# Batch 0's last values ahead of gate 9, and two of their scalings on GpSimd

## Chip, core and metric

The kernel runs on one core of a Trainium2 chip. The metric is the device time of one execution in microseconds (us). Engines are named as in the profile: PE (matmul) with PEld (its weight loads), DVE (vector), ACT (scalar), POOL or GpSimd, SP (sync). ACT, SP and GpSimd also issue DMAs.

## What is computed

Attention in which a query sees 8 global keys and the 96 keys up to its own position, with a linear bias by distance, feeds a feed-forward block (SwiGLU). Cut to what matters:

```python
# q, k, v: (4 batches, 8 heads, 768 positions, 64), float32
scores = q @ k.T / sqrt(64) - slope[head] * dist      # outside the window: -1e9
a = exp(scores - max); a = a / sum(a)
x = (a @ v) -> (3072 tokens, 512)                     # heads side by side
g = x @ w_gate                                        # 512 x 1536
out = (g * sigmoid(g) * (x @ w_val)) @ w_out          # 1536 x 512
```

## The kernel before

**Tiles.** The 3072 tokens are eight tiles t of 384; batch b gives tiles 2b and 2b+1 (its two halves). Heads go in pairs (`hp` 0 to 3) and quads (`g` 0 and 1: pairs 0 and 1, pairs 2 and 3). Of a half, every quad needs its denominators (`den`: ones times the exponentials `at`), two numerators (`num`: values `vS` times `at`, one for each `side`), and then the scaling `xT = ns * rb`, where `ns` is ACT's copy of `num` and `rb` the spread reciprocal of `den`. The four slices of `xT` (index 2g + side) are the input of the feed-forward block of that tile.

**Feed-forward.** For each f of 12, *gate f* is four matmuls (`gps`, line 560 with `wg`, one for each slice of `xT`, in order); ACT makes `th`, DVE makes `sl` from `th` and `gps` (line 576). *Value f* is four matmuls (`vps`, line 560 with `wv`), and DVE makes `hT` from `vps` and `sl` (line 580). Output products (`ops`, line 592) come in four parts of three f each, and part p reads the p-th load of the third weights, `wo`.

**Order.** The order is written out by hand. Each engine carries out its instructions in the order of the program. For tile 0 it is the list `tile0`: a pair (f, 0) is gate f, (f, 1) value f, other entries are steps. DVE's work for later is kept in the list `later`; `run_later(n)` takes n pieces from it, mostly one ahead of each gate or value. `vas(0, 1)` calls `both_values(0, 1)`: denominators of both quads (each with DVE's transpose `dT`, line 462, and reciprocal), four numerators with ACT's copies (line 525), and four pieces for `later`: `spread_first` (quad 0's `rb`, line 468, and its two scalings, line 529), `spread` (quad 1's `rb`) and two `scale` (quad 1's scalings). For batch 0, all four scalings stand on DVE; for later batches, `spread_first` puts its two on GpSimd.

**PSUM banks.** Products of tile 0 rotate over three banks (`spare`: x0, x1, x2), attention over four (`bank`: a0 to a3). `widen` puts the four a-banks ahead of the three, and `narrow`, at tile 1, gate 2, takes them back. A bank is written again only when its reader, on DVE or ACT, is done.

**Queues.** All casting loads are issued by GpSimd, in program order, on one queue; each issue takes some 0.7 to 1 us of GpSimd and waits for the load issued eight before it. Ahead of tile 0's list, `late_loads` issues thirteen: the third part of `wo` (output weights 6 to 8), the global rows of k and v (`kG`, `vG`), the fourth part of `wo`, batch 1's second half of k and q (`kst`, `qst`), and batch 1's seven loads of v. Batch 2's loads follow from tile 1 on (`stage_rows`, `load_rows`). SP issues the copies from `vG` and `kG`, the transposes and the stores of the output.

Of the kernel before, what the change touches and what calls it, by code (L numbers as in the profile page):

```python
# [37 lines left out]
def kernel(  # L38
# [12 lines left out]
    nc = tc.nc  # L51
# [97 lines left out]
    def load_qk(b, h0, h1):  # L149
        for st, src in ((kst[b], k), (qst[b], q)):  # L150
            nc.gpsimd.dma_start(
                out=st[:, h0:h1, :],
                in_=src[b, h0:h1].rearrange("h (p j) d -> p h (j d)", p=128))
# [13 lines left out]
    def load_v_rest(b, c):  # L167
        n = min(KC, S - KC * c)
        nc.gpsimd.dma_start(  # L169
            out=vSs[b][NG:NG + n, c, :, :],  # L170
            in_=v[b, :, KC * c:KC * c + n, :].rearrange("h p d -> p h d"))
# [5 lines left out]
    def load_globals():  # L177
        for dst, src in ((kG, k), (vG[:, 1:], v)):
            nc.gpsimd.dma_start(
                out=dst.rearrange("p b h d -> p (b h) d"),  # L180
                in_=src[1:, :, 0:NG, :].rearrange("b h p d -> p (b h) d"))
# [33 lines left out]
    def load_wo(g):  # L215
        nc.gpsimd.dma_start(
            out=wo[:, 3 * g:3 * g + 3, :],
            in_=moe_w_out[384 * g:384 * g + 384].rearrange("(f p) d -> p f d", p=128))
# [11 lines left out]
    state = {"tags": ["a0", "a1", "a2", "a3"], "n": 0, "x": ["x0", "x1", "x2"]}  # L230

    def bank(name, dt=FP32):
        tag = state["tags"][state["n"] % len(state["tags"])]
        state["n"] += 1
        return single(name, tag, dt)

    def banks(name, dt=FP32):
        return [bank(name, dt) for _ in range(2)]

    def spare(name, dt=FP32):  # L240
        tag = state["x"][gv.get("n", 0) % len(state["x"])]
        gv["n"] = gv.get("n", 0) + 1
        return single(name, tag, dt)
# [11 lines left out]
    def run_later(n):  # L255
        for _ in range(n):
            if later:
                later.pop(0)()
# [254 lines left out]
    def both_values(b, half):  # L513
        two = [quads[b, g] for g in range(2)]
        for quad in two:
            den = spare("den") if b > 0 else bank("den")
            quad.weigh(half, den, None)
            quad.invert(den)
        srcs = {}
        for g, quad in enumerate(two):  # L520
            for side in range(2):
                num = spare("num") if b == 0 and g == 1 else bank("num")
                quad.weigh(half, num, side)
                src = sb2.tile([128, TB], FP32, name="ns", tag="ns", bufs=4)
                nc.scalar.copy(out=src, in_=num[:, 0:TB])  # L525
                srcs[g, side] = src

        def scale_num(eng, g, side):
            eng.tensor_mul(two[g].x_out(half, side), srcs[g, side], two[g].rb)  # L529

        def spread_first():
            two[0].spread()
            for side in range(2):
                scale_num(nc.gpsimd if b > 0 else nc.vector, 0, side)

        later.append(spread_first)
        def spread():
            two[1].spread()

        later.append(spread)  # L540
        for side in range(2):
            def scale(side=side):
                scale_num(nc.vector, 1, side)

            later.append(scale)
# [3 lines left out]
    gv = {}  # L549
# [157 lines left out]
    def late_loads():  # L707
        load_wo(2)
        load_globals()
        load_wo(3)  # L710
        load_qk(1, 4, 8)
        for c in range(NCH):
            load_v_rest(1, c)

    late_loads()

    gv["n"] = 1
    hb = [bank("gps") for _ in range(4)]

    def first_gates(*terms):  # L720
        for c, f in terms:
            products(0, f, 0, c, c + 1, hb[f])
# [20 lines left out]
    def vas(b, half):  # L743
        return lambda: both_values(b, half)
# [4 lines left out]
    def trh(h0, h1, by_pair):  # L749
        def step():  # L750
            b0, b1 = single("trs", "o0", FP16), spare("trs", FP16)
            (a, b), (c, d) = [(t[:, 0:TB], t[:, TB:2 * TB]) for t in (b0, b1)]
            if by_pair:
                jobs = [(h0, (b, a), A, A), (h1, (d, c), V, V)]
            else:
                jobs = [(h0, (c, a), V, A), (h1, (d, b), V, V)]
            for hp, tr, _, _ in jobs:
                pairs[0, hp].turn_half(1, tr)
            for hp, tr, k_eng, q_eng in jobs:
                pairs[0, hp].copy_half(1, tr, k_eng, q_eng)  # L760
        return step

    def sch(hp):
        def step():
            p = pairs[0, hp]
            for which in range(2):
                p.scores_half(1, which, banks("sc"), which == 1 and hp == 2, True)
            if hp == 2:
                later.insert(0, later.pop(1))
        return step  # L770
# [46 lines left out]
    first_gates(*[(c, f) for f in range(4) for c in range(2)])  # L817
    first_gates((2, 0), (2, 1), (2, 2), (3, 0), (3, 1), (2, 3), (3, 2), (3, 3))
    def late_widen():
        widen()  # L820

    def out_next():
# [2 lines left out]
    tile0 = [(0, 0), (1, 0), (2, 0), (3, 0), trh(0, 1, True), first_val(0), first_val(1),  # L825
             bias_of(0, 0), bias_of(0, 1), scores_of(0), (0, 1), (1, 1), (2, 1),
             trh(2, 3, False), sch(1), (3, 1), (4, 0), (5, 0), sch(2), (6, 0), (4, 1), (5, 1),
             (6, 1), sch(3), (7, 0), (7, 1), (8, 0), (9, 0), vas(0, 1), late_widen, (10, 0), (8, 1),
             (11, 0), (9, 1), (10, 1), out_next, (11, 1)]

    def ff(t, f0, f1, n_out=(0,)):
# [22 lines left out]
    for b, base, rate, v_at in ((2, 20, 2.0, (31, 32, 33, 34, 35, 36, 37)), (3, 38, 1.4, (56, 57, 58, 59, 60, 61, 62))):  # L854
        items = [(base, lambda b=b: stage_rows(b)), (base + 1, lambda b=b: load_ends(b))]
        n = 0
# [11 lines left out]
    def widen():  # L868
        x, n = state["x"], gv["n"]
        state["x"] = ([state["tags"][(state["n"] + i) % 4] for i in range(4)]  # L870
                      + [x[(n + i) % 3] for i in range(3)])
        gv["n"] = 0

    def narrow():
        assert gv["n"] % 7 == 3
        state["x"] = state["x"][4:]
        state["n"] += 3
        gv["n"] = 0

    at_step(1, 2, narrow)  # L880

    def take(step_list):
# [79 lines left out]
```

## Time and profile before

| | |
|---|---|
| median of 4 runs | 239.66 us (239.24 to 239.8) |
| profiled execution, its own time | 239.80 us |
| its span in the profile | 238.0 us |
| PE busy | 231.9 us, 97% |
| DVE, ACT, POOL busy | 169.7, 127.4, 94.0 us |
| granted PE clock | full throughout |
| one scaling (line 529) on DVE, on GpSimd | 556 ns, 994 ns |

How to read it: times in the profile are in us from the start of the span. In a timeline line, the first number is the start, the second the duration of the merged group, then engine, line of the code, operation, output <- inputs, shapes, and the count (x4). In brackets stands how long the engine was idle ahead of it, and what ended that. The rows of page part 2 are forty slices of the span, each digit tenths of busy time.

### The profile page before, as it was taken

The page shows a single profiled execution, that of the slowest core. Times are in us where ns is not written, and L with a number is a line of the kernel's source. Part 1 is how long each engine was busy: PE and PEld are TensorE (multiplying, and loading weights), DVE is VectorE, ACT ScalarE, POOL GpSimd, SP SyncE. Part 2 cuts the span into 40 slices and gives each one's busy share as a digit, 9 for nine tenths or more (in the row PEclk, how much of TensorE's full clock was granted, in tenths as well). Part 3 has the DMA queues.
Part 4 walks back from the last instruction along what each step waited for, and adds up shares of the span by engine and source line. Part 5 has one row for each costly group of instructions (what it writes and reads, how often), then busy time and mean ns, then how long its engine had stood idle before and what let it go on. Part 6 is the DMA issues. An engine that isn't in the chain of part 4 may idle for free.

```text
span 238.0 us, 6012 instructions
## 1 busy us (share of the span) xinstructions
PE 231.9 (97%) x2406; PEld 134.1 (56%) x2406; DVE 169.7 (71%) x372; ACT 127.4 (54%) x290; POOL 94.0 (39%) x113
## 2 busy tenths in 40 slices
PE   7999999999999999999999999999999999999994
PEld 4665465655555556555655556555655566555543
DVE  6878889968896778676884768685885568555530
ACT  4886775687837275367347275367346526233311
POOL 8976574665990004993082063600032213000000
PEclk9999999999999999999999999999999999999999
DMA  7999999999999346999049459910010110111022
GB/s 138 171 195 200 186 200 204 196 165 160 156 152 142 97 113 93 132 134 147 4 66 114 108 113 131 134 50 21 27 44 5 42 44 3 45 47 44 8 81 90
DMA packets 83332, 25.00 MB, mean 105 GB/s; under 512 B 72600, under 2 KB 80360, under 8 KB 83304
## 3 DMA queue, kind: packets, MB, share of 16 engines
q0 software_dynamic: 64208, 14.05, 68.5%
q1 hardware_dynamic: 18664, 10.36, 17.5%
q8 instruction: 19, 0.31, 0.5%
q10 hardware_dynamic: 432, 0.21, 0.4%
q14 instruction: 9, 0.07, 0.1%
HBM read 28.62 MB, written 6.29 MB: 147 GB/s over the span
## 4 chain that ended last, share of the span: by engine, by line
PE 87%; DMA 7%; POOL 3%; ACT 1%; issue 0%; DVE 0%; POOLq 0%
PE gps L560 26%; PE vps L560 25%; PE ops L592 25%; DMA wg<-in_moe_w_gate_dram 7%; PE num L452 3%; PE sc L392 3%; PE den L452 2%; PE trs L272 1%; POOL vS L169 1%; PE ops L608 1%; POOL k L118 1%; ACT at L367 1%; POOL q L118 1%; POOL wg L211 0%; PE sc L356 0%
## 5 line engine op out<-in xcount | busy, mean ns | idle before, releaser
L571 ACT ACTIVATE th<-gps 128x384 f32<-128x384 f32 x96 | 47.3, 494 | 61.8 <-PE gps L560 57.2
L560 PE MATMUL gps<-xT,wg 128*128 128x384 f16 x384 | 78.0, 327 | 1.0 <-DMA wg<-in_moe_w_gate_dram 0.3
L576 DVE SCALAR_TENSOR_TENSOR sl<-th,gps 128x384 f32<-128x384 f32 x96 | 52.7, 551 | 36.7 <-ACT th L571 36.1
L560 PE MATMUL vps<-xT,wv 128*128 128x384 f16 x384 | 77.6, 326 | 0.3 <-DMA wv<-in_moe_w_val_dram 0.3
L592 PE MATMUL ops<-wo,hT 128*128 128x512 f16 x276 | 73.1, 379 | 0.0
L580 DVE TENSOR_TENSOR hT<-vps,sl 128x384 f16<-128x384 f32 x96 | 52.8, 554 | 7.8 <-PE vps L560 0.6
L560 PEld LDWEIGHTS <-wg 128*128 128x128 f16 x384 | 35.4, 98 | 32.6 <-issue 2.7
L560 PEld LDWEIGHTS <-wv 128*128 128x128 f16 x384 | 37.2, 98 | 26.0 <-DMA wv<-in_moe_w_val_dram 0.9
L592 PEld LDWEIGHTS <-hT 128*128 128x128 f16 x276 | 26.9, 98 | 23.7
L400 ACT ACTIVATE at<-sc 128x432 f16<-128x432 f32 x72 | 33.9, 533 | 10.3 <-PE sc L392 10.3
L529 POOL TENSOR_TENSOR xT<-ns,rb 128x384 f16<-128x384 f32 x10 | 9.8, 996 | 63.4 <-ACT ns L525 32.1
L169 POOL DMA_DIRECT2D vS<-in_v_dram x28 | 24.8, 899 | 4.7 <-DMA kst<-in_k_dram 2.0
L598 ACT ACTIVATE osb<-ops 128x512 f32<-128x512 f32 x23 | 13.7, 597 | 14.3 <-PE ops L592 14.1
L411 POOL TENSOR_TENSOR at<-at,masks 128x864 f16<-128x864 f16 x4 | 7.3, 1821 | 23.9 <-ACT at L400 19.3
L411 DVE TENSOR_TENSOR at<-at,masks 128x864 f16<-128x864 f16 x20 | 12.2, 609 | 5.4 <-ACT at L400 5.4
L192 POOL DMA_DIRECT2D kst<-in_k_dram x16 | 14.1, 901 | 3.5 <-DMA vS<-in_v_dram 2.4
L525 ACT COPY ns<-num 128x384 f32<-128x384 f32 x24 | 9.8, 494 | 9.9 <-PE num L452 9.9
L192 POOL DMA_DIRECT2D qst<-in_q_dram x16 | 13.8, 889 | 0.3 <-PE trs L272 0.3
L367 ACT ACTIVATE at<-sc 128x432 f16<-128x432 f32 (+2 forms) x32 | 11.4, 462 | 1.5 <-PE sc L356 1.5
L408 DVE TENSOR_TENSOR at<-at,masks 128x432 f16<-128x432 f16 x24 | 8.1, 377 | 4.1 <-ACT at L400 4.1
L452 PE MATMUL num<-at,vS 128*32 128x216 f16 (+6 forms) x576 | 10.9, 224 | 0.0
L462 DVE STREAM_TRANSPOSE dT<-den 128x384 f32<-128x384 f32 x16 | 9.3, 581 | 1.2 <-PE den L452 0.5
(72 smaller groups left out, 164.9 us busy)
## 6 DMA issues: line engine op xcount, KB each, us to landing
out_dram<-osb SPq DMA_DIRECT2D x23, 256.0 KB
vS<-in_v_dram POOLq DMA_DIRECT2D x24, 120.0 KB, 5.4
wg<-in_moe_w_gate_dram POOLq DMA_DIRECT2D x6, 256.0 KB, 9.5
wv<-in_moe_w_val_dram POOLq DMA_DIRECT2D x6, 256.0 KB, 8.2
wo<-in_moe_w_out_dram POOLq DMA_DIRECT2D x4, 384.0 KB, 10.2
qst<-in_q_dram POOLq DMA_DIRECT2D x16, 96.0 KB, 4.3
kst<-in_k_dram POOLq DMA_DIRECT2D x16, 90.0 KB, 4.4
kst<-in_k_dram POOLq DMA_DIRECT2D x2, 384.0 KB, 10.8
```

The costliest lines, as they stand in the source:

```text
L169: nc.gpsimd.dma_start(out=vSs[b][NG:NG + n, c, :, :], in_=v[b, :, KC * c:KC * c + n, :].rearrange("h p d -> p h d"))
L192: nc.gpsimd.dma_start(out=st[b][p0:p0 + n, h // 2, :, h % 2, :], in_=src[b, h, 0:n * J].rearrange("(t p) d -> p t d", p=n))
L367: nc.scalar.activation(out=at[:, hi, 0:col + n], in_=sc[hi][:, 0:col + n], func=AF.Exp, scale=scale)
L400: nc.scalar.activation(out=at[:, hi, :], in_=sc[hi][:, 0:BANK], func=AF.Exp, scale=scale)
L411: mul_eng.tensor_mul(at, at, m[:, :, o:o + BANK])
L452: nc.tensor.matmul(dst[r, o:o + n], lhsT=ones[:, 0:32] if side is None else vals[:, 4 * g + j, side::2], rhs=pairs[b, 2 * g + j // 2].at[c ...
L560: nc.tensor.matmul(gv[f, which][:, 0:TB], lhsT=w[:, c, 128 * f:128 * f + 128], rhs=x_of(t)[:, c, :], start=(c == 0), stop=(c == NC - 1))
L571: nc.scalar.activation(out=th, in_=dst[:, 0:TB], func=AF.Tanh, scale=0.5)
L576: nc.vector.scalar_tensor_tensor(out=sl, in0=th, scalar=1.0, in1=dst[:, 0:TB], op0=AluOp.add, op1=AluOp.mult)
L580: nc.vector.tensor_mul(hTs[t][:, f, :], dst[:, 0:TB], gv.pop(("sl", f)))
L592: nc.tensor.matmul(ops, lhsT=hTs[t][:, f, 128 * i:128 * i + 128], rhs=wo[:, f, :], start=(f == 0), stop=(f == NFF - 1))
L598: nc.scalar.mul(out=osb, in_=ops, mul=0.5)
```

## The change

Three things move. In `spread_first`, the two scalings of quad 0 are given to GpSimd for batch 0 as well. `late_loads()` is no longer called ahead of tile 0's list, but in `late_widen`, after `run_later(1)` has issued `spread_first`; on GpSimd the thirteen loads therefore stand behind the two scalings. In `tile0`, gate 9 moves from ahead of `vas(0, 1)` to behind `late_widen`, so that PE carries out denominators and numerators right after gate 8. As one product less is on the three banks by then, and one more on the seven, `narrow` counts four used banks instead of three.

```diff
         def spread_first():
             two[0].spread()
             for side in range(2):
-                scale_num(nc.gpsimd if b > 0 else nc.vector, 0, side)
+                scale_num(nc.gpsimd, 0, side)
...
-    late_loads()
-
...
     def late_widen():
+        run_later(1)
+        late_loads()
         widen()
...
-             (6, 1), sch(3), (7, 0), (7, 1), (8, 0), (9, 0), vas(0, 1), late_widen, (10, 0), (8, 1),
+             (6, 1), sch(3), (7, 0), (7, 1), (8, 0), vas(0, 1), late_widen, (9, 0), (10, 0), (8, 1),
...
     def narrow():
-        assert gv["n"] % 7 == 3
+        used = gv["n"] % 7
+        assert used <= 4
         state["x"] = state["x"][4:]
-        state["n"] += 3
+        state["n"] += used
         gv["n"] = 0
```

In the built program, DVE's order after gate 8's `sl` becomes: `dT` and reciprocal of both quads, both spreads, gate 9's `sl`, a scaling of quad 1, gate 10's `sl`, the other scaling, value 8's `hT`. On GpSimd an instruction of the library (profiled as MODIFY_POOL_CONFIG), which the build places ahead of the first multiply on that engine, moves with it: before, it stands ahead of batch 1's scalings, behind the third load of batch 2's v; after, ahead of batch 0's scalings, behind the first half of batch 1's q.

## The prediction

> **What bounds the kernel now.** I read the page first (busy time, slices), then the timeline around the edit, then GpSimd's own timeline and the rows of line 529.
>
> ```profile
> PE 231.9 (97%) x2406; PEld 134.1 (56%) x2406; DVE 169.7 (71%) x372; ACT 127.4 (54%) x290; POOL 94.0 (39%) x113
> ...
> PEclk9999999999999999999999999999999999999999
> DMA  7999999999999346999049459910010110111022
> ```
>
> PE is the bound, at full clock; the other engines matter only where PE waits for them. The DMA engines are full until about 77 us. The timeline from 30 to 40 us:
>
> ```profile
> 30.62 0.81 PE L560 MATMUL gps<-xT,wg 128*128 128x384 f16 x4
> ...
> 31.16 0.55 DVE L576 SCALAR_TENSOR_TENSOR sl<-th,gps 128x384 f32<-128x384 f32 x1 [0.43 <-ACT th L571]
> ...
> 31.63 0.60 DVE L373 TENSOR_TENSOR at<-at,masks 128x864 f16<-128x864 f16 x1
> 31.77 0.81 PE L560 MATMUL gps<-xT,wg 128*128 128x384 f16 x4 [0.33 <-DVE sl L576]
> ...
> 32.51 0.79 PE L452 MATMUL den<-at,ones 128*32 128x72 f16 x40
> ...
> 32.62 1.07 DVE L576 SCALAR_TENSOR_TENSOR sl<-th,gps 128x384 f32<-128x384 f32 x2
> ...
> 33.13 1.39 PE L452 MATMUL num<-at,vS 128*32 128x72 f16 x80
> ...
> 34.45 0.82 PE L560 MATMUL gps<-xT,wg 128*128 128x384 f16 x4
> ...
> 34.55 0.58 DVE L462 STREAM_TRANSPOSE dT<-den 128x384 f32<-128x384 f32 x1
> ...
> 35.19 0.81 PE L560 MATMUL vps<-xT,wv 128*128 128x384 f16 x4
> ...
> 37.95 1.03 DVE L529 TENSOR_TENSOR xT<-ns,rb 128x384 f16<-128x384 f32 x2
> ...
> 39.08 0.81 PE L560 MATMUL gps<-xT,wg 128*128 128x384 f16 x4
> ```
>
> Gate 8 is at 30.62, gate 9 at 31.77, gate 10 at 34.45, value 8 at 35.19, tile 1's first gate at 39.08. Four matmuls take 0.65, so PE was ready for gate 9 at 31.27 and stood 0.50 us: its bank was gate 7's, which DVE's sl frees at 31.71. That is all the idle time to be won here. From 34.45 on PE has next to no gap.
>
> GpSimd's timeline, then the rows of line 529 on GpSimd:
>
> ```profile
> 32.02 0.74 POOL L151 DMA_DIRECT2D qst<-in_q_dram  x1
> 32.75 0.74 POOL L216 DMA_DIRECT2D wo<-in_moe_w_out_dram  x1
> ...
> 41.20 0.95 POOL L169 DMA_DIRECT2D vS<-in_v_dram  x1 [1.25 <-DMA kst<-in_k_dram]
> 43.12 0.94 POOL L169 DMA_DIRECT2D vS<-in_v_dram  x1 [0.98 <-DMA qst<-in_q_dram]
> 44.98 3.58 POOL L169 DMA_DIRECT2D vS<-in_v_dram  x4 [0.92 <-DMA wo<-in_moe_w_out_dram]
> ```
>
> ```profile
> L529 POOL TENSOR_TENSOR xT<-ns,rb x10: 992/994/1002, 92.6 to 199.0; 128x384 f16<-128x384 f32 x10
> ...
> L529 POOLq MODIFY_POOL_CONFIG  x2: 112/112/113, 71.3 to 71.3; - x2
> ```
>
> Two things to see. Each load waits for the one issued eight before it, so the right-hand notes date landings: kst of 31.11 by 41.20, qst of 32.02 by 43.12, wo of 32.75 by 44.98. At 32.75 some 10 us of transfers stand in line. And ahead of GpSimd's first multiply of the whole program stands a library load, two MODIFY_POOL_CONFIG at 71.3, as soon as the issues before it are out (71.4). The first multiply comes at 92.58, so 21 us cover it.
>
> [...]
>
> **The change part by part.**
>
> *Gate 9 behind the values.* The stall of 0.50 goes, and two others take its place. After gate 8 PE goes straight to the denominators: 31.27 plus the change-over (0.09: 32.51 against 31.77 + 0.65), 31.36. Quad 0's twenty take 0.31, the first ten of quad 1's 0.12: 31.80. The eleventh reads pair 3's second half, whose mask (31.63 + 0.60) is ready at 32.23. Before, PE came there at 32.95, too late to notice; now it stands until 32.28, with all 80 numerators and gate 9 queued behind. The last ten end at 32.47, the 80 numerators take 1.32: gate 9 starts at 33.79 in the bank of quad 0's denominator. DVE frees that in time: one sl instead of two (0.52 less) lies ahead of its transposes, so they run at 33.09 and 34.03 instead of 33.61 and 34.55. Gate 10 takes quad 1's bank, free at 34.61: PE, ready at 34.45, starts at 34.67, and value 8 at 35.33, against 35.19. **Sum: 0.14 us late**, give or take 0.1. Nor could more be won: value 8's second half of weights lands only at 35.1 to 35.4 (GpSimd's wait for it ended ahead of 35.41), and its third matmul starts at 35.51 now, so at most 0.35 of gain.
>
> *Bank bookkeeping.* Seven banks in another rotation, four used instead of three: no instruction, and each bank's last reader is over by then. 0.
>
> *Two scalings from DVE to GpSimd.* DVE is spared 2 x 0.55, from 35.9. No PE wait lies there (its ones are in time even now: 37.95 + 1.03 against 39.08), so 0. On GpSimd they need quad 0's spread, ready at 35.31 (0.52 earlier than 35.83), and ACT's copies, earlier too: 35.4 to 37.35 if nothing else holds them. PE needs the first at 39.22, the second with the next matmul at 39.38: 2 us of room.
>
> *The library load.* In the built order of the changed kernel it stands ahead of these scalings, behind the qst issue of 32.02. So it starts at 32.76, and the 21 us of cover become 2.6. With a length L the scalings end at 32.76 + L + 1.95, and PE, 0.05 later, loses 32.76 + L + 2.00 - 39.38 = **L - 4.62**. From both sides: nothing up to 4.6[...]. I take 8.5[...]: **3.9 us**.[...] PE is 97% busy and back to back afterwards, so nothing gives this back.
>
> *The loads issued behind.* wo's third part, kG, vG, wo's fourth, the second kst and qst, seven vS, with batch 2's rows behind them, go from 32.75 to behind the scalings: 37.35 without the load, 43.2 at L = 8.5. The line of transfers lasts to about 43, so in the first case nothing lands later: the wait for eight before holds vS at 41.20 anyway. In the second the line runs dry and landings move by some 2.5 us; readers move by 4. wo's third part is read at 46.5 now, 1.8 after landing (44.7 to 45). 0, as long as PE is later than the transfers. SP's copies from vG wait until 50.35 anyway.
>
> *Sum.* 0.14 + 3.9 = 4.0 on the profiled execution's 239.80, 243.84. That execution stands 0.14 above the median of 239.66, so I forecast **243.7**.
>
> **Rivals.**
>
> 1. *Not slower: the library load is short, or done ahead.* For it: nothing in the records shows its length, and the first multiply at 92.58 starts in the moment its inputs are there. Against: that was 21 us later, which says nothing below 21. It decides at L = 4.6 us. Then only gate 9's move is left, between 0.35 won and 0.25 lost: 239.3 to 239.9, likeliest 239.8.
>
> 2. *No library cost, but late weights hold PE.* If a transfer takes its 12 us from issue (32.75 to 44.98) instead of its place in line, wo's third part, issued at 37.35, lands at 49.6 and PE, which reads it at 46.5, loses 3.1: 242.9. Against: the landings are 1.9 us apart, as in a line.
>
> 3. *DVE is the hidden bound and the 1.1 us come back.* Against: from 34.45 PE runs without gaps, so there is nothing to take; at most rival 1's lower end.
>
> **How the numbers follow.** A measurement here tells about 0.2%, 0.5 us, from no change. The library load in the open[...]: 0.78, times of 241.1 to 248.8. Rival 1: 0.14, nearly all within 0.2%. Rival 2: 0.05. Rival 3 or faster for a reason not seen: 0.03. So slower 0.83, same 0.13, faster 0.04.[...]
>
> **What would show it.** Right: MODIFY_POOL_CONFIG near 32.8, the first line 529 on GpSimd at about 41 and not 35.4; PE's gate of tile 1 waiting for POOL xT L529 by some 4 us; denominators stopped by the mask of line 373 near 32.3; value 8 near 35.3. Wrong: scalings at 35.4 (no library cost), or a PE wait for DMA wo at 46 to 50 (rival 2), or PE idle elsewhere.

## The result and the profile after

The changed kernel takes 240.01 us (median of 43 runs, 239.37 to 240.54) against 239.61 for the kernel before (64 runs): a ratio of **1.0014, interval 1.0008 to 1.002**. It is slower, but by about 0.34 us by that ratio (the two medians are 0.40 apart), and not by the 4 us of the forecast. The profiled execution took 239.95 us with a span of 238.2.

The page of the changed kernel, busy time and the DMA slices:

```profile
PE 231.7 (97%) x2406; PEld 134.2 (56%) x2406; DVE 169.4 (71%) x370; ACT 127.7 (54%) x290; POOL 96.3 (40%) x115
...
DMA  8999999999999474999049459910010110111022
```

PE does the same 2406 matmuls and its share is unchanged. The DMA slices differ from those of before in the first one and from 77 to 95 us (4, 7, 4 tenths instead of 3, 4, 6), where PE's digits stay at 9. The loss is too small for the page. It is seen in the timeline of the changed kernel around the edit (start, duration, engine, line, operation, count, idle time ahead and its releaser):

```profile
30.46 0.81 PE L560 MATMUL gps<-xT,wg 128*128 128x384 f16 x4
...
31.20 0.69 PE L452 MATMUL den<-at,ones 128*32 128x72 f16 x30
...
32.12 0.34 PE L452 MATMUL den<-at,ones 128*32 128x216 f16 x8 [0.23 <-DVE at L373]
...
32.33 1.11 PE L452 MATMUL num<-at,vS 128*32 128x72 f16 x61
...
33.65 0.45 PE L452 MATMUL num<-at,vS 128*32 128x192 f16 x15 [0.20 <-issue]
...
34.03 1.47 PE L560 MATMUL gps<-xT,wg 128*128 128x384 f16 x8
...
35.29 2.27 POOL L529 TENSOR_TENSOR xT<-ns,rb 128x384 f16<-128x384 f32 x2 [2.19 <-DVE rb L468]
35.34 0.81 PE L560 MATMUL vps<-xT,wv 128*128 128x384 f16 x4
...
37.51 0.79 POOL L216 DMA_DIRECT2D wo<-in_moe_w_out_dram  x1
...
39.24 0.81 PE L560 MATMUL gps<-xT,wg 128*128 128x384 f16 x4
```

Gate 8 itself starts at 30.46 here and at 30.62 before: its time differs by some tenths from profile to profile (29.93 to 30.62 in all of them). So I read everything as time after gate 8, written with a plus sign. Gate 9 starts at +3.57, value 8 at +4.88 (before +4.57), tile 1's first gate at +8.78 (before +8.46). **The loss of 0.31 us is complete at value 8 and only carried from there.** The lines show two stops on the way: the denominators wait for the mask of line 373 until 32.12, and the last 15 numerators start at 33.65, after a stop that no engine and no transfer ends ("issue").

The rows of line 529 on GpSimd, changed kernel (duration min/median/max in ns, first and last start):

```profile
L529 POOL TENSOR_TENSOR xT<-ns,rb x12: 991/996/1307, 35.3 to 199.1; 128x384 f16<-128x384 f32 x12
...
L529 POOLq MODIFY_POOL_CONFIG  x2: 37/37/37, 33.1 to 33.1; - x2
```

The scalings run at 35.29, with MODIFY_POOL_CONFIG, the library load of the forecast, at 33.1 ahead of them. There is no load in the open, which was the main term of the forecast: the wait of 2.19 ahead of the scalings ends with `rb`.

### The profile page after: what moved, and what is told of

It reads as the page before. It is cut to its first block, busy times and chain, and to the rows that moved or that the text cites. A ratio compares the mean times of both kernels' runs of the same rounds, so it can differ in the third digit from the quotient of the medians.

```text
span 238.2 us, 6015 instructions
## 1 busy us (share of the span) xinstructions
PE 231.7 (97%) x2406; PEld 134.2 (56%) x2406; DVE 169.4 (71%) x370; ACT 127.7 (54%) x290; POOL 96.3 (40%) x115
## 4 chain that ended last, share of the span: by engine, by line
PE 87%; DMA 7%; POOL 3%; ACT 1%; issue 1%; DVE 0%; POOLq 0%
PE gps L560 26%; PE vps L560 25%; PE ops L592 25%; DMA wg<-in_moe_w_gate_dram 7%; PE num L452 4%; PE sc L392 3%; PE den L452 2%; PE trs L272 1%; POOL vS L169 1%; PE ops L608 1%; POOL k L118 1%; ACT at L367 1%; POOL q L118 1%; POOL wg L211 0%; PE sc L356 0%
## 5 line engine op out<-in xcount | busy, mean ns | idle before, releaser
L560 PEld LDWEIGHTS <-wg 128*128 128x128 f16 x384 | 35.4, 98 | 32.0 <-issue 2.1
L529 POOL TENSOR_TENSOR xT<-ns,rb 128x384 f16<-128x384 f32 x12 | 12.1, 1022 | 65.6 <-DVE rb L468 54.7
```

Of the source, the lines that this page charges most:

```text
L560: nc.tensor.matmul(gv[f, which][:, 0:TB], lhsT=w[:, c, 128 * f:128 * f + 128], rhs=x_of(t)[:, c, :], start=(c == 0), stop=(c == NC - 1))
```

## The experiments

The theories after this result: **T1**, the loss is gate 9's move alone, through the two stops; **T2**, the scalings or the loads issued behind them cost something; **T3**, MODIFY_POOL_CONFIG does start a load that takes its time, but it hides between 33.1 and 35.29.

### Each half alone

e1_gate_only undoes what was done to GpSimd, e2_gpsimd_only what was done to gate 9.

```diff
 # e1_gate_only, against the changed kernel
-                scale_num(nc.gpsimd, 0, side)
+                scale_num(nc.gpsimd if b > 0 else nc.vector, 0, side)
...
+    late_loads()
...
         run_later(1)
-        late_loads()
         widen()
```

> Only gate 9 moves behind batch 0's last values; the two scalings stay on DVE and the thirteen loads keep their old place. Theory (the order on PE is the whole loss): as slow as the full change, 1.0014 of before (0.2 to 0.5 us), with gate 9 starting about 3.6 us after gate 8 and value 8 about 4.9 us after it (4.57 before), a hold in the denominators at the mask of line 373, and a stop of about 0.3 us inside the last numerator. Rival (GpSimd's scalings, its library instruction or the later loads are the loss): no slower than before, within 0.1 us.

```diff
 # e2_gpsimd_only, against the changed kernel
-             (6, 1), sch(3), (7, 0), (7, 1), (8, 0), vas(0, 1), late_widen, (9, 0), (10, 0), (8, 1),
+             (6, 1), sch(3), (7, 0), (7, 1), (8, 0), (9, 0), vas(0, 1), late_widen, (10, 0), (8, 1),
```

> Only the scalings go to GpSimd and the loads behind them; gate 9 stays ahead of the values. Theory (order on PE is the loss, GpSimd and loads are hidden): within 0.1 us of before, scalings start as soon as quad 0's rb is ready, PE has the stall of 0.5 us ahead of gate 9 and no stop in the numerators. Rival (late loads or GpSimd cost something): 0.2 to 0.4 us slower than before, with a PE wait for POOL xT or for DMA wo.

Measured: e1 1.0013 [1.0003, 1.0024], e2 0.9993 [0.9984, 1.0003]. PE's timeline in e1:

```profile
30.22 0.81 PE L560 MATMUL gps<-xT,wg 128*128 128x384 f16 x4
...
33.38 0.45 PE L452 MATMUL num<-at,vS 128*32 128x192 f16 x15 [0.17 <-issue]
33.77 1.47 PE L560 MATMUL gps<-xT,wg 128*128 128x384 f16 x8
```

Gate 9 at +3.55 and value 8 at 35.08, +4.86: e1 repeats the changed kernel's numbers with both stops in it, the one in the last 15 numerators too. In e2 value 8 is at +4.57 and tile 1's gate at +8.46, as before. So the whole loss is gate 9's move; scalings and loads on GpSimd cost nothing that can be measured (at the upper end of e2's interval, 0.07 us). T2 falls.

### The library load

Two multiplies of ones are put on GpSimd directly behind batch 1's first half of q, ahead of the scalings, so that they need nothing that could hide a load.

```diff
 # e3_lib_probe, against the changed kernel
     load_qk(1, 0, 4)
+    probe = sb.tile([128, 2, 64], FP16, name="probe")
+    for i in range(2):
+        nc.gpsimd.tensor_mul(probe[:, i], ones[:, 0:64], ones[:, 64:128])
```

> The full change with two more small multiplies (128x64, of a constant tile, result unused) on GpSimd, right behind the library instruction and ahead of the scalings; their input is ready since the start, so the time from MODIFY_POOL_CONFIG to the first of them is the library load itself, with the DMA engines full. If the load is long but hidden in the change by the wait for rb: the first multiply starts 1 to 2.2 us after MODIFY_POOL_CONFIG. If nothing is loaded: within 0.3 us. If the first call is what costs: it is much longer than the second.[...]

One run, 239.95 us. The rows of the added line on GpSimd in e3:

```profile
L708 POOLq MODIFY_POOL_CONFIG  x2: 37/37/37, 33.4 to 33.4; - x2
L708 POOL TENSOR_TENSOR probe<-ones x2: 309/312/316, 33.5 to 33.7; 128x64 f16<-128x64 f16 x2
```

The first multiply follows the two MODIFY_POOL_CONFIG within 0.1 us, and the two take the same time (309 to 316 ns). T3 falls: in this program nothing of that length stands behind the instruction.

### The stop in the numerators

The stop has no releaser, and it stands at the same place, 15 numerators ahead of gate 9, in the changed kernel, in e1, in e3 and below in e5. That points at the instructions themselves. Page part 3 has 19 packets of 16 KB in a DMA queue of kind "instruction" (q8): here instructions arrive in blocks. I took this queue to be PE's, whose 2 x 2406 records would then be some 253 to a packet, an estimate from the page; e4 tests it. If PE ran out of instructions, moving the block's border by other instructions should remove the stop, or move it. e4 makes 44 short warm-up products of 12 long ones: 64 more PE instructions (a weight load and a matmul for each of 32 more products), at the start of the program.

```diff
 # e4_shift, against the changed kernel
-            nc.tensor.matmul(warm[:, 0:256], lhsT=ones[:, 0:128], rhs=ones[:, 0:256],
+            nc.tensor.matmul(warm[:, 0:64], lhsT=ones[:, 0:128], rhs=ones[:, 0:64],
...
-    fill(12)
+    fill(44)
```

> The full change with the 12 warm-up matmuls of 256 columns at the start cut into 44 of 64 columns: same array time, but 64 more instructions ahead on PE, so every later 16 KB packet of PE's instruction stream[...] starts 64 instructions earlier in the work. Theory (the stop inside the last numerator is PE waiting for its next packet of instructions): the stop of 0.3 us goes, or moves to another place; gate 9 comes about 0.3 us earlier after gate 8 (3.3 us), gate 10 then waits some 0.2 us for DVE's dT of quad 1, and the whole is 0.1 to 0.2 us faster than the full change. Rival (the stop belongs to the numerators themselves, a bank or a value load): it stays where it was, gate 9 at 3.6 us after gate 8.

Measured: 239.67 us, ratio 1.0003 [0.9988, 1.0018]. The interval holds both the time of before and that of the changed kernel, so the reading rests on the trace. The timeline of e4:

```profile
30.23 0.81 PE L560 MATMUL gps<-xT,wg 128*128 128x384 f16 x4
...
32.10 1.38 PE L452 MATMUL num<-at,vS 128*32 128x72 f16 x76
...
33.42 1.66 PE L560 MATMUL gps<-xT,wg 128*128 128x384 f16 x8
...
34.92 0.81 PE L560 MATMUL vps<-xT,wv 128*128 128x384 f16 x4
```

The last 76 numerators go through in 1.38, without a stop. Gate 9 starts at +3.19, gates 9 and 10 take 1.66 instead of 1.47 because gate 10 now waits for quad 1's `dT`, and value 8 is at +4.69. The DMA view of the stretch from 29 to 34 us in the changed kernel, and then of 24 to 29 us in e4 (packets, MB, share):

```profile
q8 instruction: 1, 0.02, 1.2%
```

```profile
q8 instruction: 1, 0.02, 1.1%
```

In the changed kernel the block's packet is on its way from 31.36 to 32.29 and the instructions taken to be its own run at 33.65; in e4 the packet is there by 26.4, and none comes from 29 to 34. This also tells whose packet it is: e4 adds instructions to PE alone, and q8's packet comes 5.9 us earlier, while the 8 KB packets of the other instruction queue (q14) keep their places near 24.5 and 30.2. It fits a block that is asked for at a fixed earlier instruction: 64 instructions of gates and values are some 5 us of PE's time (eight of them take 0.65), those of denominators and numerators less than one. The kernel before has the late packet as well (to 32.36), but PE comes to that place only at about 34.0, 1.7 after the packet's end, and does not notice. Why the instructions run only 1.4 us or more after their packet's end, the runs don't show.

To know what the same edit does to the kernel before, it was run there too.

> The kernel before with the warm-up in 44 pieces alone: control. There PE reaches row 962 of its instructions later than their packet, so nothing is to be won: ratio 1.000 within 0.001, value 8 at 4.57 us after gate 8. If cutting the warm-up gains by itself (an earlier start), it shows here and has to be taken off the two kernels above.

e8_before_shift: 239.52 us, 1.0003 [0.999, 1.0016], value 8 at +4.56 and tile 1's gate at +8.46. So what e4 has over the changed kernel at value 8 (+4.69 against +4.88) comes with the stop and not from the warm-up as such. These are single profiles: e3, the changed kernel with a shorter stop, has value 8 at +4.77.

### Taking the stops away one by one

e5 gives DVE pair 3's second mask one item earlier, ahead of gate 7's `sl`; e6 adds e4's edit; e7 also gives gate 9 the bank of gate 8, so that gate 10 no longer waits for quad 1's `dT`.

```diff
 # e5_mask_first, against the changed kernel
             run_later(3)
+        elif item == (7, 0):
+            run_later(2)
 # e7_mask_shift_rot: also e4's edit, and in widen and narrow
-        state["x"] = ([state["tags"][(state["n"] + i) % 4] for i in range(4)]
-                      + [x[(n + i) % 3] for i in range(3)])
+        xs = [x[(n + i) % 3] for i in range(3)]
+        state["xs"] = xs[1:] + xs[:1]
+        state["x"] = (xs[:1] + [state["tags"][(state["n"] + i) % 4] for i in range(4)]
+                      + xs[1:])
...
-        state["x"] = state["x"][4:]
-        state["n"] += used
+        state["x"] = state["xs"]
+        state["n"] += used - 1
```

> The full change with pair 3's second mask (line 373) one piece earlier in DVE's order, ahead of gate 7's sl, so that it is ready before PE's denominators reach it. If the hold at the mask were a loss by itself, gate 9 would come 0.4 us sooner after gate 8 (3.57 us in the full change). Expected instead: the hold goes and nothing is gained, gate 9 again at 3.4 to 3.6 us after gate 8, since the last loads of batch 0's values (vS, landing near 32.2 and 32.4) stop the first numerator and PE's instructions from row 962 on stop the last one, as before.

PE's timeline in e5 (one run, 239.79 us), with two lines of its weight loads (PEld) in between:

```profile
31.02 0.79 PE L452 MATMUL den<-at,ones 128*32 128x72 f16 x40
...
32.00 0.10 PEld L452 LDWEIGHTS <-vS 128*32 128x32 f16 x4 [0.21 <-DMA vS<-in_v_dram]
...
32.26 0.75 PEld L452 LDWEIGHTS <-vS 128*32 128x32 f16 x49 [0.15 <-DMA vS<-in_v_dram]
...
33.40 0.45 PE L452 MATMUL num<-at,vS 128*32 128x192 f16 x15 [0.22 <-issue]
33.78 1.47 PE L560 MATMUL gps<-xT,wg 128*128 128x384 f16 x8
```

The wait for the mask is gone: 40 denominators in 0.79. Gate 8 was at 30.28, and gate 9 is still at +3.50, as expected. PE comes to the numerators about 0.4 earlier and loses it again in two places: the loads of `vS`, the values of batch 0, end two short waits (0.21 and 0.15), and PE then stands before the same instruction as in the changed kernel, 0.46 from one numerator's start to the next instead of 0.40. The three lie one behind the other, and taking the first away brings out the next.

> The same with the warm-up in 44 pieces, so that no packet of instructions is missing in the numerators. Expected: no stop in the last numerator, a short wait of the first numerator for vS, gate 9 about 3.05 us after gate 8; gate 10 then waits for DVE's dT of quad 1 and value 8 stays at about 4.6 to 4.7 us. If the packets were not the cause of the stop in the last numerator, gate 9 stays at 3.4 or later.

PE's timeline in e6 (one run, 239.35 us):

```profile
32.21 1.29 PE L452 MATMUL num<-at,vS 128*32 128x168 f16 x68 [0.53 <-DMA vS<-in_v_dram]
33.43 1.47 PE L560 MATMUL gps<-xT,wg 128*128 128x384 f16 x8
```

Both stops are gone, and I had expected gate 9 near +3.05. It came at +3.50, and value 8 at +4.81 instead of 4.6 to 4.7: a miss. By the sign on record (gate 9 at 3.4 or later) it would even speak against the packets; but the last 68 numerators run through without a stop. The bracket names the reason ahead of them, a wait of 0.53 for a load of `vS`. Gate 8 was early in this run (29.93), the loads were not.

> The same, and the seven banks begin with the free one of the three, so that gate 9 takes gate 8's bank, gate 10 the bank of quad 0's denominators and value 8 that of quad 1's: no gate waits for the second dT. All three waits of the full change are then gone. Expected: gate 9 at 3.05, gate 10 at 3.7, value 8 at 4.3 to 4.4 us after gate 8, 0.2 us ahead of before (4.57): ratio 0.999. If something else on PE takes its place, value 8 is at 4.5 or later and the time is that of before.

Measured: 239.72 us, 1.0004 [0.9993, 1.0014]. PE's weight loads in e7:

```profile
31.82 0.17 PEld L452 LDWEIGHTS <-vS 128*32 128x32 f16 x12
32.15 0.10 PEld L452 LDWEIGHTS <-vS 128*32 128x32 f16 x4 [0.16 <-DMA vS<-in_v_dram]
32.43 0.96 PEld L452 LDWEIGHTS <-vS 128*32 128x32 f16 x64 [0.18 <-DMA vS<-in_v_dram]
33.49 1.09 PEld L560 LDWEIGHTS <-wg 128*128 128x128 f16 x8
```

Again the numerators wait for `vS`, here twice, and the last 64 can't start ahead of 32.43. Gate 9 is at +3.01 and value 8 at +4.32, as expected, 0.25 better than before when counted from gate 8. The expected ratio of 0.999 did not come. Gate 8 was at 30.48, and on the clock of the span hardly anything is won: value 8 starts at 34.80 (34.74 in e6, 34.92 in e4, 34.88 in e8, the kernel before with the warm-up alone). That the loads, which keep their own time, set this limit is argued from these traces and was not tested. No version beats the kernel before beyond its interval. An earlier load of `vS` wasn't tried; it would stand ahead of weights that PE also waits for.

## Why the prediction was wrong

**The step that failed is the library load.** It was set at 8.5 us in the open, of which PE was to lose 3.9. e3 measures at most 0.1 us. The 8.5 us were my assumption: no trace of this case showed that MODIFY_POOL_CONFIG loads anything, or for how long. Ahead of a plain multiply, which the profile calls TENSOR_TENSOR, e3 shows no such price, and the measurement decides. Whether the instruction loads anything at all, the runs don't show. The prediction had written "nothing in the records shows its length" and still gave the load 0.78 of the chances. The case of a short load was seen and kept as rival 1 with 0.14. Its mechanism came true: scalings at 35.29 where the "if nothing else holds them" branch said 35.4. Its time did not quite: 0.34 us above before, where rival 1 reached 0.25.

**Gate 9's move: right mechanism, size off.** The hold at the mask was to last until 32.28 - 30.62 = 1.66 after gate 8; it did, 32.12 - 30.46 = 1.66. The term that was mis-sized is "80 numerators take 1.32": in the changed kernel PE stopped for 0.40 within them, which e4 puts down to missing instructions, and gate 9 came at +3.57 instead of +3.17. The prediction had no term for the arrival of instructions. With that stop out of the way, e4 meets the working to 0.02: gate 9 at +3.19, value 8 at +4.69, where the prediction has 33.79 - 30.62 = 3.17 and 35.33 - 30.62 = 4.71. The stop of 0.40 took the place of gate 10's predicted wait of 0.22 for `dT`, so value 8 is late by 0.31 instead of 0.14: 0.14 + 0.40 - 0.22 = 0.32.

**The bound on what could be won held, but another limit came first.** The prediction limited the gain to 0.35 by value 8's late weights; the most that any run shows is e7's 0.25 after gate 8, and none of it in the time. e5, e6 and e7 show an earlier limit that it didn't name: the numerators wait for the loads of `vS`.

**The terms set at nothing were nothing.** For DVE's spared scalings and GpSimd's added ones, e2 shows 0.9993, with 1 inside the interval. The bank bookkeeping, which e2 doesn't touch, shows no wait: tile 1's first gate starts 3.90 after value 8, and 3.89 before. The loads issued behind start at 37.51 (predicted 37.35 for the case without a load). wo's third part lands at 45.20, against 44.69 before, and no wait for it appears, so rival 2 is out. GpSimd's two scalings took 2.27 instead of the 1.95 of the working, and PE, with 2 us of room there, did not wait for them. Rival 3 is out too: e2 spares DVE the same work and gains nothing clear of noise.

## What to carry to other kernels

A gap between two instructions that something else covers says nothing about the cost of the first; before such a cost is given a size, let it also be zero, and measure it with a few small instructions that depend on nothing. Where a move packs many short PE instructions together, check that the next block of instructions has come: here its packet ended at 32.29, PE stood for 0.40 ahead of 33.65, and with the packet 5.9 us earlier (e4) there was no stop. A wait with "issue" beside it is a reason to look only where it stands at one fixed instruction in every run and moves or goes when instructions are added ahead of it; "issue" alone stands beside some forty other gaps of PE's weight loads in the changed kernel. When an order by hand is shifted to close one gap, list what is late next (here mask, values of v, instructions, `dT`), since each took the place of the one removed.

## What the runs showed of the hardware

*PE seems to have run short of instructions.* From one numerator's start to the next, the stop was 0.40 us in the changed kernel, 0.37 in e1, 0.24 in e3 and 0.46 in e5, each time at the same numerator and 1.4 to 1.6 us after the end of the 16 KB packet. It was in none of the three runs of the new order with 64 PE instructions more (e4, e6, e7); the kernel before has it neither with them (e8) nor without. That the packet belongs to PE is worked out from e4, where it comes 5.9 us earlier, and not recorded.

*GpSimd and DVE seem to slow each other when both scale.* GpSimd's second scaling of batch 0 in the changed kernel:

```profile
36.26 1.31 POOL L529 TENSOR_TENSOR xT<-ns,rb 128x384 f16<-128x384 f32 x1
```

It takes 1307 ns (1296 in e2, 1323 in e3) where the other eleven take 991 to 1003. It runs beside parts of DVE's two scalings of quad 1, which take 0.75 and 0.88 us in the changed kernel, 0.75 and 0.89 in e3 and 2.02 together in e2, where the kernel before has 0.55 to 0.56 for each of its four and 1.03 for two together. DVE's `sl` at the same time, which reads PSUM, kept its 0.52 to 0.54. GpSimd's first scaling, which meets DVE's for only 0.33 us, took 1.00, so the slow one isn't the first call. Why, the traces don't show, and no run isolated it.
